# Linear attention with a SwiGLU FFN: another first load, corner matmuls and a new order of loads and attention steps in the first groups

## The chip, the cores and the metric

The kernel runs on one core of a Trainium2 chip. The metric is the device time of one execution in microseconds, lower is better. The kernel before takes 308.3 us, the median of 7 runs (307.77 to 308.72).

## The reference

q, k and v have 8 batches, 8 heads, 576 rows and 64 columns, all fp32. The output of a linear attention is laid out as 4608 tokens of 512 features and goes through a gated FFN with d_ff = 1536.

```python
q_p, k_p = phi(q), phi(k)                     # phi(x) = where(x > 0, x, exp(x) - 1) + 1
kv  = einsum('bhsd,bhse->bhde', k_p, v)
z   = sum(k_p, axis=2)
num = einsum('bhsd,bhde->bhse', q_p, kv)
den = einsum('bhsd,bhd->bhs', q_p, z)[..., None] + 1e-06
x   = (num / den).transpose(0, 2, 1, 3).reshape(4608, 512)
g   = x @ w_gate
out = (silu(g) * (x @ w_val)) @ w_out
```

## The kernel before

**Tiling.** A batch's 576 rows are 9 chunks j of 64 rows. A group g is 8 consecutive chunks (b, j), 512 tokens; there are 9 groups for the 8 batches, so group 0 holds chunks 0 to 7 of batch 0, and group 1 the last chunk of batch 0 and seven of batch 1. The kernel overlaps the attention of later batches with the FFN of a group. `lp` is a half of the heads (four heads, two SBUF pairs); `hh` and `e` pick 64-row halves of the array. d_ff is 12 blocks `fb` of 128.

**FFN.** L1 of a group computes, per fb, four gate matmuls and four value matmuls of 128x512 (`l1_mm`, lines 289 to 292), then ACT's silu and one DVE product into `hT` (`l1_gate`, 294 to 298). L2 multiplies hT with `wo` (line 450 for groups 0 and 1; line 506 for the later ones, which work on sums of weights `ws` and of hT; line 343 for the last two). `w_sum` (486) makes the weight sums, on POOL for the first blocks and on DVE in L1 of group 1.

**PSUM.** There are eight banks of 128x512 fp32: pG0-1, pV0-2, pX0-2. `l1_banks` (283) says which hold gate and value results; group 0 rotates four pairs, later groups two gate and three value banks.

**Attention of batch 0 (prologue, 680 to 713).** phi is kept as two terms, max(x, 0) and min(exp(x), 1), which are added by DVE (`k_sum`) for the first half of k only; elsewhere PE adds them in PSUM. `z0` sums phi(k) over rows with a ones matrix, `z0_copy` brings it to `zz`. `t0` transposes phi(q) by matmuls with an identity, `t0_copy` brings it to `qT`. `mm1` (166) computes v.k: for batch 0 in matmuls of 64 rows by 128 columns, of which two 64x64 blocks are used, for batch 1 as 64x64 corners. `r0_copies` (650) brings it to `R`, and `kv` (200) finds the blocks there. `corners` (258) multiplies zz or R with qT. `den0` takes logarithms and exponentials of the denominators on ACT; `num0` (671) multiplies numerators by them on DVE (`x0`, two products of 128x512) into `xT`, the FFN's input. The eight last-chunk (j = 8) products of batch 0, called d8 and n8, come in lines 856 to 869. `warm` (590) are matmuls without a use that keep PE running.

**Attention of batch 1 (first(), 796 to 808).** In L1 of group 0, after fb 3 a `block` computes exp and both terms of phi(k) for batch 1, and after fb 8 one for phi(q). The rest stands in lists between L2's steps: `t1` transposes phi(q), four and three chunks at a time with both head halves together, then `z0`, `den1`, `mm1`, `num1`, and for the last two chunks `t1(7, 9)`, `den2`, `num2`, `x2`. Some phi work of batch 2 stands there too (`exp_k`, `max_2`, `phi_k`, `exp_q`).

**What sets the order.** Everything is issued in the order of the program text to each engine's own queue; there is no planner. `at` (728) puts functions into numbered slots. All loads of q, k, v and the weights are DMAs issued by POOL that change fp32 to fp16 on the way; a half of q, k or v of batch 0 is 288 KB in fp16, a whole one 576 KB, a W1 block of 256 columns 256 KB for gate and the same for value, a third of wo 512 KB. They land in the order of issue. Outputs and transposes are DMAs of SyncE (SP).

The first loads are lines 570 to 577 (k half 0, q halves 0 and 1, k half 1, v halves, W1 columns 0 to 255), the next ones lines 714 to 725. The first L1 of group 0 for fb 0 and 1 is interleaved by contraction block i (lines 848 to 852), because xT 0 and 1 are there before xT 2 and 3:

```python
for i in range(4):
    for w in range(2):
        for fb in range(2):
            l1_mm(0, fb, w, i)
    if i == 0:
        r0_copies(1)
        num0(1)
```

L2 of group 0 (881 to 892) takes four fb for each of four token tiles t, three times.

Of the kernel before, what the change touches and what calls it, by code (L numbers as in the profile page):

```python
# [17 lines left out]
def kernel(  # L18
# [90 lines left out]
    def ld_w1(c0, c1):  # L109
        for (src, dst) in ((moe_w_gate, wg), (moe_w_val, wv)):  # L110
            nc.gpsimd.dma_start(out=dst[:, :, c0:c1], in_=src[:, c0:c1].rearrange("(c p) f -> p c f", p=P))

    def ld_w2(i):
        nc.gpsimd.dma_start(out=wo[:, 4 * i:4 * i + 4, :],
                            in_=moe_w_out[512 * i:512 * i + 512, :].rearrange("(c p) f -> p c f", p=P))
# [50 lines left out]
    def mm1(b, lp):  # L166
        if lp == 0:
            kvb[b] = ((pV[2], pX[0]), (pX[2], pV[2]), (pX[0], pX[1]), (pV[0], pG[0]), (pX[2], pV[2]))[min(b, 4)]
        for j in range(J):
            for (t, term_) in enumerate(terms_k(b, lp)):  # L170
                for hh in range(2):
                    rows = slice(C * hh, C * hh + C)
                    if b == 0:
                        nc.tensor.matmul(
                            out=kvb[b][hh][:, 256 * lp:256 * lp + P], lhsT=term_[rows, j, P * lp:P * lp + P],
                            rhs=v16[b][rows, 2 * lp:2 * lp + 2, D * j:D * j + D],
                            start=(j == 0 and t == 0), stop=(j == J - 1 and t == len(terms_k(b, lp)) - 1))
                        continue
                    for e in range(2):
                        w = D if b == 1 else D + 1  # L180
                        nc.tensor.matmul(  # L181
                            out=kvb[b][hh][D * e:D * e + D, 256 * lp:256 * lp + w],
                            lhsT=term_[rows, j, P * lp + D * e:P * lp + D * e + D],
                            rhs=v16[1][rows, 2 * lp + e, D * j:D * j + D] if b == 1 else vm[b % 2][rows, j, 2 * lp + e, :],
                            start=(j == 0), stop=(j == J - 1))
# [14 lines left out]
    def kv(b):  # L200
        c1 = D if b == 0 else 0
        return lambda i, e: R[b % 2][D * e:D * e + D, i, c1 * e:c1 * e + D]
# [80 lines left out]
    def l1_banks(g, fb):  # L283
        if g > 0:
            return pG[fb % 2], pV[fb % 3]
        i = fb % 4
        return (pG[0], pG[1], pX[0], pX[1])[i], (pV[0], pV[1], pV[2], pX[2])[i]
# [282 lines left out]
    load_0(k, k16, 0)  # L570
# [6 lines left out]
    ld_w1(0, 256)  # L577
# [25 lines left out]
    def k_max(lp):  # L603
        term(k16[0], kp[1], lp, 0.0, ALU.max)
# [14 lines left out]
    zb0 = (pG, (pX[2], pV[2]))  # L619

    def z0(b, lp):
        ts = terms_k(b, lp)
        for j in range(J):
            for t in ts:
                for hh in range(2):
                    rows = slice(C * hh, C * hh + C)
                    nc.tensor.matmul(out=zb0[b][hh][:, D * lp:D * lp + D], lhsT=t[rows, j, P * lp:P * lp + P],
                                     rhs=ones[rows, 0:D], start=(j == 0 and t is ts[0]),
                                     stop=(j == J - 1 and t is ts[-1]))

    def z0_copy(b, lp):
        for hh in range(2):
            nc.vector.tensor_scalar(out=zz[:, 2 * lp + hh, :], in0=zb0[b][hh][:, D * lp:D * lp + D], scalar1=1.0 / SC,
                                    scalar2=None, op0=ALU.mult)
# [15 lines left out]
    def r0_copies(lp):  # L650
        for hh in range(2):
            nc.vector.tensor_copy(out=R[0][:, 2 * lp + hh, 0:P], in_=kvb[0][hh][:, 256 * lp:256 * lp + P])
# [18 lines left out]
    def num0(lp):  # L671
        corners({2 * lp + e: nbank0[lp][e][:, :] for e in range(2)}, kv(0), 0, 0, 8, (lp,))
        for i in range(2 * lp, 2 * lp + 2):
            x0(nbank0[lp][i % 2][:, :], rr[:, i, :], xT[i][0][:, :])

    def t0_all(lp, t):
        for i in range(2):
            t0(pV[i], lp, 4 * i, 4 * i + 4, (t,))

    warm(42, pX[1])  # L680
    exp0(k16[0], ek, 0)
# [7 lines left out]
    z0_copy(0, 0)  # L689
    t0_all(0, 0)  # L690
    warm(2, pX[1])
    q_min(0)
    q_max(0, 1)
# [4 lines left out]
    warm(7, pX[1])  # L698
    den0(0)
    q_min(1)  # L700
    k_max(1)
    t0_all(1, 0)
    t0_all(1, 1)
    t0_copy(pV[0], 1, 0, 4, V)
# [3 lines left out]
    t0_copy(pV[1], 1, 4, 8, V)  # L708
# [5 lines left out]
    for c in (256, None, 512, 768, 1024):  # L714
        if c is None:
            ld_k(1)
        else:
            ld_w1(c, c + 256)
    ld_q(1)
    ld_w1(1280, 1536)  # L720
    ld_w2(0)
    ld_v(1)
    ld_w2(1)
    ld_w2(2)
# [9 lines left out]
    def phi_1(src, e, dst, lp):  # L734

        s = slice(2 * lp, 2 * lp + 2)
        nc.vector.tensor_scalar(out=e[:, s, :], in0=e[:, s, :], scalar1=1.0, scalar2=None, op0=ALU.min)
        d = dst[1][:, :, P * lp:P * lp + P].rearrange("p j (s d) -> p s j d", d=D)
        nc.vector.tensor_tensor(out=d, in0=d, in1=e[:, s, :].rearrange("p s (j d) -> p s j d", d=D), op=ALU.add)

    def t1(ps, j0, j1, eng):
        pt = ps[:, :].bitcast(FP16)
        for jj in range(j1 - j0):
            for lp in range(2):
                i = 2 * jj + lp
                nc.tensor.transpose(out=pt[:, P * i:P * i + P], in_=qp[1][:, j0 + jj, P * lp:P * lp + P],
                                    identity=id16[:, :])
        dst = qT[1][:, j0:j1, :, :].rearrange("p j l t -> p (j l t)")
        if eng == "A":
            nc.scalar.activation(out=dst, in_=pt[:, 0:2 * P * (j1 - j0)], func=AF.Copy, bias=0.0, scale=1.0)  # L750
        else:
            nc.vector.tensor_copy(out=dst, in_=pt[:, 0:2 * P * (j1 - j0)])
# [9 lines left out]
    def num1(lp):  # L762
        corners({2 * lp + e: nbank[e][:, 0:W7] for e in range(2)}, kv(1), 1, 0, 7, (lp,))
        for e in range(2):
# [8 lines left out]

    def num2():
        corners([nbank[m % 2][:, part1[m]] for m in range(4)], kv(1), 1, 7, 9)

    def x2():
        for m in range(4):
            x0(nbank[m % 2][:, part1[m]], r8[:, m % 2, part1[m]], xT[m][0][:, 0:W2])
# [6 lines left out]
    def block(src, e, dst):  # L786
        for lp in range(2):
            exp_(src, e, 1, lp)
            term(src[1], dst[1], lp, 0.0, ALU.max)
        for lp in range(2):  # L790
            phi_1(src, e, dst, lp)
# [4 lines left out]
    def first():  # L796
        sl = at(FB, [
            (3, lambda: block(k16, ek, kp)), (8, lambda: block(q16, eq, qp))])
        ln_set = lambda: nc.scalar.preload_act_table_set("natural_log_exp_and_others")
        w = at(13, [  # L800
            (0, lambda: t1(pX[0], 0, 4, A)), (0, ln_set), (1, lambda: t1(pX[1], 4, 7, V)), (1, lambda: z0(1, 0)),
            (1, lambda: z0(1, 1)), (1, lambda: z0_copy(1, 0)), (1, lambda: z0_copy(1, 1)),
            (2, lambda: den1(0)), (2, lambda: mm1(1, 0)), (2, lambda: mm1(1, 1)), (2, lambda: r1_copies()),
            (3, lambda: den1(1)), (3, lambda: num1(0)), (5, lambda: t1(pX[0], 7, 9, V)), (5, lambda: num1(1)),
            (6, lambda: den2()), (6, lambda: exp_k(2, 0)), (6, lambda: exp_k(2, 1)), (7, lambda: max_2(k16, kp, 0)),
            (7, lambda: max_2(k16, kp, 1)), (8, lambda: num2()), (9, lambda: phi_k(2, 0)), (9, lambda: exp_q(2, 0)),
            (11, lambda: exp_q(2, 1)), (12, lambda: x2()), (12, lambda: phi_k(2, 1))])
# [39 lines left out]
    part8 = [slice(C * (i // 2), C * (i // 2) + C) for i in range(4)]  # L847
    for i in range(4):
# [3 lines left out]
        if i == 0:  # L852
            r0_copies(1)
            num0(1)
        if i == 1:
            for lp in range(2):
                t0(pV[2][:, P * lp:P * lp + P], lp, 8, 9)
            for lp in range(2):
                t0_copy(pV[2][:, P * lp:P * lp + P], lp, 8, 9, V)
        if i == 2:  # L860
            d8 = [(pV[2], pX[0])[m % 2][:, part8[m]] for m in range(4)]
            n8 = [(pX[1], pX[2])[m % 2][:, part8[m]] for m in range(4)]
            corners(d8, zs, 0, 8, 9)
            ln0([pV[2][:, 0:P], pX[0][:, 0:P]], r8[:, :, 0:P])
            exp_neg(r8[:, :, 0:P])
    nc.scalar.preload_act_table_set("silu_and_others")
    corners(n8, kv(0), 0, 8, 9)
    for m in range(4):
        x0(n8[m], r8[:, m % 2, part8[m]], xT[m][1][:, 0:C])
# [11 lines left out]
    for i in range(3):  # L881
        if i < 2:
            for m in range(4):
                w_sum(nc.gpsimd, m, 2 * i, 2 * i + 2)
        for t in range(4):
            l2(0, t, 4 * i, 4 * i + 4)
            if (i, t) == (2, 1):
                l2_out(0, 1, V)
            for f in w[4 * i + t]:
                f()  # L890
            if i == 2 and t != 1:
                l2_out(0, t, V)
    for f in w[12]:
        f()
# [90 lines left out]
```

## Time and profile before

| | us |
|---|---|
| median of 7 runs (lowest, highest) | 308.3 (307.77, 308.72) |
| the profiled execution | 308.19 |
| its span in the trace | 306.4 |
| start of the first L1 matmul (line 291) | 16.38 |
| fb 2 of L1, group 0 | 21.76 |
| L2 of group 0 | 39.21 |
| L1 of group 1 | 54.13 |
| L2 of group 1 | 76.19 |
| L1 of group 2 | 87.74 |

The landings of the first loads, taken from the trace as the time when the last of the 16 DMA engines reports, in us:

| load | issued | landed |
|---|---|---|
| k half 0 | 1.26 | 5.40 |
| q half 0 | 2.12 | 8.03 |
| q half 1 | 3.13 | 9.47 |
| k half 1 | 3.84 | 10.90 |
| v halves | 4.55, 5.26 | 12.34, 13.76 |
| W1 0:256, gate and value | 6.03, 6.77 | 15.09, 17.44 |
| W1 256:512 | 7.50, 8.31 | 18.39, 19.73 |
| k(1) | 9.75 | 22.57 |
| W1 512:1280 | 11.19 to 18.68 | 23.92 to 30.59 |
| q(1) | 20.01 | 33.45 |
| W1 1280:1536 | 22.86, 24.20 | 34.79, 36.13 |
| wo 0:4 | 25.54 | 38.70 |
| v(1) | 26.87 | 41.50 |
| wo 4:8 and 8:12 | 28.23, 29.55 | 44.06, 46.72 |

Times in the trace count from the start of the span; the profiled execution's own time is longer than the span by what lies before its first and after its last instruction. The stages in the first table are where PE starts the named work; between two of them PE runs that stage and whatever attention work is put between its matmuls. Stages after 87.74 hold nothing that the diff changes.

### The profile page before, as it was taken

The page shows a single profiled execution, that of the slowest core. Times are in us where ns is not written, and L with a number is a line of the kernel's source. Part 1 is how long each engine was busy: PE and PEld are TensorE (multiplying, and loading weights), DVE is VectorE, ACT ScalarE, POOL GpSimd, SP SyncE. Part 2 cuts the span into 40 slices and gives each one's busy share as a digit, 9 for nine tenths or more (in the row PEclk, how much of TensorE's full clock was granted, in tenths as well). Part 3 has the DMA queues.
Part 4 walks back from the last instruction along what each step waited for, and adds up shares of the span by engine and source line. Part 5 has one row for each costly group of instructions (what it writes and reads, how often), then busy time and mean ns, then how long its engine had stood idle before and what let it go on. Part 6 is the DMA issues. An engine that isn't in the chain of part 4 may idle for free.

```text
span 306.4 us, 6673 instructions
## 1 busy us (share of the span) xinstructions
PE 298.5 (97%) x2587; PEld 183.2 (60%) x2587; DVE 251.2 (82%) x537; ACT 216.5 (71%) x335; POOL 48.3 (16%) x62
## 2 busy tenths in 40 slices
PE   8899999999999999999999999999999999999993
PEld 6644454444454486447744774468446888878882
DVE  3757757979977988998899889997999968968991
ACT  3759987969757878696869686968633478547930
POOL 8545386010200002000200000000000004001300
PEclk9999999999999999999999999999999999999999
DMA  7999999999496219921792133122312050033014
GB/s 100 194 199 199 203 207 208 258 215 165 67 226 131 49 28 161 213 51 29 128 238 47 36 69 71 28 54 52 87 26 54 10 131 0 2 68 72 0 37 103
DMA packets 41424, 32.29 MB, mean 105 GB/s; under 512 B 16352, under 2 KB 37280, under 8 KB 41392
## 3 DMA queue, kind: packets, MB, share of 16 engines
q0 software_dynamic: 20672, 18.94, 39.1%
q1 hardware_dynamic: 20560, 12.79, 17.8%
q8 instruction: 20, 0.33, 0.5%
q10 hardware_dynamic: 160, 0.13, 0.2%
q14 instruction: 12, 0.10, 0.1%
HBM read 37.75 MB, written 9.44 MB: 154 GB/s over the span
## 4 chain that ended last, share of the span: by engine, by line
PE 86%; issue 5%; DMA 3%; POOL 2%; ACT 2%; POOLq 0%; ACTq 0%
PE pV L291 22%; PE pG L291 21%; PE pX L506 14%; PE pV L506 4%; PE pV L343 4%; PE pG L343 4%; PE pG L450 4%; PE pV L450 3%; DMA wv<-in_moe_w_val_dram 3%; PE pX L291 3%; PE pX L343 1%; PE pV L264 1%; PE pX L181 1%; PE pV L411 1%; PE pX L264 1%
## 5 line engine op out<-in xcount | busy, mean ns | idle before, releaser
L291 PE MATMUL pV<-xT,wv 128*128 128x512 f16 x324 | 83.5, 379 | 0.5 <-DMA wv<-in_moe_w_val_dram 0.5
L291 PE MATMUL pG<-xT,wg 128*128 128x512 f16 x312 | 80.4, 379 | 0.1
L296 ACT ACTIVATE sil<-pG 128x512 f16<-128x512 f32 x78 | 45.9, 596 | 27.7 <-PE pG L291 18.0
L297 DVE SCALAR_TENSOR_TENSOR hT<-pV,sil 128x512 f16<-128x512 f32 x81 | 55.1, 687 | 12.0 <-ACT sil L296 7.0
L291 PEld LDWEIGHTS <-wv 128*128 128x128 f16 x336 | 32.8, 98 | 40.4 <-DMA wv<-in_moe_w_val_dram 1.0
L291 PEld LDWEIGHTS <-wg 128*128 128x128 f16 x336 | 32.2, 98 | 38.3 <-issue 0.7
L506 PEld LDWEIGHTS <-hs 128*128 128x128 f16 x336 | 32.5, 98 | 4.7 <-DVE hs L480 0.4
L383 POOL TENSOR_TENSOR hT<-prod,vm 128x512 f16<-128x512 f16 x6 | 6.9, 1153 | 132.0 <-ACT vm L370 132.0
L506 PEld LDWEIGHTS <-hT 128*128 128x128 f16 x252 | 24.3, 98 | 4.1
L506 PE MATMUL pX<-ws,hs 128*128 128x256 f16 x210 | 25.7, 273 | 0.0
L511 ACT ACTIVATE part<-pX 128x256 f32<-128x256 f32 x35 | 12.8, 381 | 13.2 <-PE pX L506 13.2
L95 POOL DMA_DIRECT2D k<-in_k_dram x7 | 5.2, 747 | 79.4 <-ACT part L511 58.8
L480 DVE TENSOR_TENSOR hs<-hT 128x512 f16<-128x512 f16 (+2 forms) x42 | 17.4, 418 | 0.2
L245 DVE TENSOR_TENSOR qp<-qp,rden 128x768 f16<-128x768 f16 x18 | 17.1, 949 | 0.0
L232 DVE TENSOR_REDUCE den<-prod 128x12 f32<-128x768 f16 x18 | 17.0, 943 | 0.0
L120 ACT ACTIVATE ek<-k 128x1152 f16<-128x1152 f16 x14 | 15.9, 1159 | 0.1
L120 ACT ACTIVATE eq<-q 128x1152 f16<-128x1152 f16 x14 | 15.6, 1168 | 0.0
L506 PE MATMUL pX<-wo,hT 128*128 128x256 f16 x126 | 15.2, 273 | 0.0
L450 PEld LDWEIGHTS <-hT 128*128 128x128 f16 x96 | 8.8, 98 | 10.3 <-issue 0.6
L155 ACT ACTIVATE vm<-v 128x1152 f16<-128x1152 f16 x12 | 14.1, 1177 | 0.0
L516 DVE SCALAR_TENSOR_TENSOR osb<-pX,part 128x256 f32<-128x256 f32 x28 | 10.7, 417 | 2.1 <-PE pX L506 1.9
L450 PE MATMUL pG<-wo,hT 128*128 128x512 f16 x48 | 11.7, 380 | 0.0
(183 smaller groups left out, 536.1 us busy)
## 6 DMA issues: line engine op xcount, KB each, us to landing
out_dram<-osb SPq DMA_DIRECT2D x64, 128.0 KB, 4.0
k<-in_k_dram POOLq DMA_DIRECT2D x7, 576.0 KB, 11.7
q<-in_q_dram POOLq DMA_DIRECT2D x7, 576.0 KB, 11.7
v<-in_v_dram POOLq DMA_DIRECT2D x7, 576.0 KB, 14.6
wg<-in_moe_w_gate_dram POOLq DMA_DIRECT2D x6, 256.0 KB, 11.7
wv<-in_moe_w_val_dram POOLq DMA_DIRECT2D x6, 256.0 KB, 11.9
wo<-in_moe_w_out_dram POOLq DMA_DIRECT2D x3, 512.0 KB, 15.8
out_dram<-osb SPq DMA_DIRECT2D x13, 64.0 KB, 2.0
```

What stands on the lines that cost most here:

```text
L120: nc.scalar.activation(out=e[:, s, :], in_=src[b % 2][:, s, :], func=AF.Exp, bias=0.0, scale=1.0)
L155: nc.scalar.activation(out=vm[b % 2][:, :, s, 0:D].rearrange("p j l d -> p l j d"), in_=v16[b % 2][:, s, :].rearrange("p l (j d) -> p l j ...
L232: nc.vector.tensor_reduce(out=den[:, HL * j0:HL * j1], in_=prod[:, 0:j1 - j0, :].rearrange("p j (l d) -> p (j l) d", d=D), axis=AX.X, op=A ...
L245: nc.vector.tensor_tensor(out=qv, in0=qv, in1=rden[:, HL * j0:HL * j1].unsqueeze(2).to_broadcast([P, HL * (j1 - j0), D]), op=ALU.mult)
L291: nc.tensor.matmul(out=ps[:, :], lhsT=src[:, i, P * fb:P * fb + P], rhs=xT[i][g % 2][:, :], start=(i == 0), stop=(i == 3))
L296: nc.scalar.activation(out=s[:, :], in_=pg[:, :], func=AF.Silu, bias=0.0, scale=1.0)
L297: nc.vector.scalar_tensor_tensor(out=hT[g % 2][:, fb, :], in0=pv[:, :], scalar=SC, in1=s[:, :], op0=ALU.mult, op1=ALU.mult)
L343: nc.tensor.matmul(out=dst[:, HN * e:HN * e + HN], lhsT=lhs, rhs=rhs, start=(n in (1, 2, 5) and e == 0 and c == 0), stop=(c == 1), skip_gr ...
L450: nc.tensor.matmul(out=pso[(g, t)][:, :], lhsT=hT[g % 2][:, fb, P * t:P * t + P], rhs=wo[:, fb, :], start=(fb == 0), stop=(fb == FB - 1))
L480: (eng or nc.vector).tensor_tensor(out=o, in0=a, in1=b, op=op)
L506: nc.tensor.matmul(out=(z if n in (2, 3, 5) else x)[:, 0:HD], lhsT=left(f), rhs=right(f), start=(f == 0 and n in (1, 2, 5)), stop=(f == HF ...
L511: nc.scalar.activation(out=part[:, 2 * i + tt, :], in_=(x if from_x else z)[:, 0:HD], func=AF.Copy, bias=0.0, scale=1.0 / SC)
```

## The change

The diff touches the loads, the attention of batches 0 and 1, and the banks of one stage.

- The first half of k is loaded by SyncE, in fp32 without a change of type, into the space of `ws` (`k32`); the exponential and the max read it there. POOL's first load is now q's first half.
- W1 columns 0 to 255 are loaded in row halves: gate rows 0:2, value rows 0:2, gate 2:4, value 2:4 (in blocks of 128 rows), four DMAs of half the size. wo is loaded as 0:2, 2:4, 4:8, 8:12.
- The later loads are in another order: W1 256 to 1279, then k(1), W1 1280, q(1), wo 0:2 and 2:4, v(1), wo 4:8, 8:12, k(2).
- Batch 0's v.k is computed as 64x64 corners like batch 1's: 108 matmuls where there were 54. The copies to R are 64 columns wide instead of 128. z0 of batch 0, the second half of t0 and the tails (j = 8) use other banks.
- In the prologue, `q_max(0, 1)` stands ahead of `q_min(0)`, the transposes of the second head half ahead of `den0(0)`, the tail transposes and copies ahead of `z0(0, 1)`; `num0` is cut into corners and `x00` products, and the R copies of the second half stand between two of them. The warm matmuls go from 51 to 41.
- The denominators of the last chunk follow `num0(1)` directly; its numerators (`num8`, `x8`) are moved into L2 of group 0.
- Batch 1's k block moves from after fb 3 to after fb 7, its q block from after fb 8 into L2 (slot 3), with exponentials written to `ws`'s space (`eq1`).
- L2 of group 0 has 16 steps instead of 12, two, two, four and four fb for each t, and the attention of batch 1 is spread over their slots. `t1` transposes one head half at a time (7 chunks), `t2` the last two chunks.
- Group 1's L1 rotates three gate banks (pG0, pG1, pX2) instead of two.

The core of the diff:

```diff
-    load_0(k, k16, 0)
+    k32 = ws[:, :, :, :].rearrange("p m f c -> p (m f c)").bitcast(FP32)[:, 0:2 * J * D].rearrange("p (l x) -> p l x", l=2)
+    nc.sync.dma_start(out=k32, in_=heads(k, 0)[:, 0:2, :])
...
-    ld_w1(0, 256)
+    ld_w1(0, 256, 0, 2)
+    ld_w1(0, 256, 2, 4)
...
-        term(k16[0], kp[1], lp, 0.0, ALU.max)
+        term(k16[0] if lp else k32, kp[1], lp, 0.0, ALU.max)
...
-                    if b == 0:
-                        nc.tensor.matmul(
-                            out=kvb[b][hh][:, 256 * lp:256 * lp + P], lhsT=term_[rows, j, P * lp:P * lp + P],
-                            rhs=v16[b][rows, 2 * lp:2 * lp + 2, D * j:D * j + D],
-                            start=(j == 0 and t == 0), stop=(j == J - 1 and t == len(terms_k(b, lp)) - 1))
-                        continue
                     for e in range(2):
-                        w = D if b == 1 else D + 1
+                        w = D if b < 2 else D + 1
...
-            return pG[fb % 2], pV[fb % 3]
+            return (pG[0], pG[1], pX[2])[fb % 3] if g == 1 else pG[fb % 2], pV[fb % 3]
...
+    q_max(0, 1)
+    q_min(0)
     t0_all(0, 0)
-    warm(2, pX[1])
-    q_min(0)
-    q_max(0, 1)
     t0_all(0, 1)
     t0_copy(pV[0], 0, 0, 4, V)
     t0_copy(pV[1], 0, 4, 8, A)
     exp0(k16[0], ek, 1)
-    warm(7, pX[1])
-    den0(0)
+    t0_all(1, 0)
+    warm(4, pX[1])
     q_min(1)
     k_max(1)
-    t0_all(1, 0)
     t0_all(1, 1)
-    t0_copy(pV[0], 1, 0, 4, V)
+    for lp in range(2):
+        t0(bank8[lp][:, 3 * P:4 * P], lp, 8, 9)
+    den0(0)
+    for i in range(2):
+        t0_copy(pG[i], 1, 4 * i, 4 * i + 4, V)
     k_min(1)
     mm1(0, 0)
     r0_copies(0)
-    t0_copy(pV[1], 1, 4, 8, V)
+    for lp in range(2):
+        t0_copy(bank8[lp][:, 3 * P:4 * P], lp, 8, 9, V)
     z0(0, 1)
     z0_copy(0, 1)
     num0(0)
     den0(1)
     mm1(0, 1)
-    for c in (256, None, 512, 768, 1024):
-        if c is None:
-            ld_k(1)
-        else:
-            ld_w1(c, c + 256)
+    x00(0, 0)
+    r0_copies(1)
+    x00(0, 1)
+    for c in (256, 512, 768, 1024):
+        ld_w1(c, c + 256)
+    ld_k(1)
+    ld_w1(1280, 1536)
     ld_q(1)
...
+        w = at(17, [
+            (3, lambda: z0(1, 0)), (3, lambda: z0(1, 1)), (3, q_block), (7, lambda: t1(0)), (7, lambda: mm1(1, 0)),
+            (7, lambda: mm1(1, 1)), (7, lambda: num8()), (7, lambda: r1_copies()), (7, lambda: x8()), (8, lambda: t1(1)),
+            (8, lambda: den1(0)), (9, lambda: num1(0)), (9, lambda: den1(1)), (9, lambda: x1(0)), (11, lambda: t2()),
+            (11, lambda: num1(1)), (11, lambda: x1(1)), (12, lambda: exp_k(2, 0)), (12, lambda: den2()),
+            (12, lambda: max_2(k16, kp, 0)), (12, lambda: max_2(k16, kp, 1)), (14, lambda: num2()),
+            (14, lambda: exp_k(2, 1)), (14, lambda: exp_q(2, 0)), (15, lambda: exp_q(2, 1)), (16, lambda: x2()),
+            (16, lambda: phi_k(2, 0)), (16, lambda: phi_k(2, 1))])
```

## The prediction

> **What bounds the kernel now.** I read the page first, then the chain of waits, then windows by stage, then the timeline of the first 20 us.
>
> ```profile
> PE 298.5 (97%) x2587; PEld 183.2 (60%) x2587; DVE 251.2 (82%) x537; ACT 216.5 (71%) x335; POOL 48.3 (16%) x62
> ...
> DMA  7999999999496219921792133122312050033014
> ```
>
> PE is busy 97% of the span, so an edit pays only if PE does less, or waits less, at a place where PE is last. The DMA row is full in its first ten slices (76 us). All that the diff touches lies there. By stage (start:end, length, then busy time of PE, PEld, DVE, ACT, POOL, clock, DMA share, GB/s):
>
> ```profile
> 16.38:21.76 5.38, 4.88 (x44) 1.86 (x40) 2.28 (x7) 2.32 (x5) 2.22 (x3) 1.00 1.33 204
> 21.76:39.21 17.45, 17.45 (x89) 7.95 (x82) 12.63 (x25) 16.42 (x20) 7.33 (x10) 1.00 1.36 201
> 39.21:54.13 14.92, 14.92 (x207) 7.34 (x206) 9.68 (x21) 12.29 (x18) 11.57 (x12) 1.00 1.22 207
> 54.13:76.19 22.06, 21.92 (x171) 10.08 (x169) 19.34 (x43) 18.39 (x27) 1.48 (x2) 1.00 1.12 217
> ```
>
> These are fb 0 and 1 of the first L1 with batch 0's corners; fb 2 to 11; L2 of group 0 with batch 1's attention; L1 of group 1. Outside the first, PE hardly idles: ten fb at 8 x 0.216 us are 17.28 of the second's 17.45. So time can come from the start (the prologue up to 16.38, where PE's 13.99 busy us are mostly warm-up matmuls, and the 5.38) or from fewer PE instructions. The chain agrees:
>
> ```profile
> 4.56 1.48 POOL v L98 x2
> 6.78 10.67 DMA wv<-in_moe_w_val_dram
> 21.84 0.97 PE pX L291 x4
> ```
>
> It begins with POOL's issues and the wv load. What else sets the start (timeline: start, duration, engine; in brackets the idle time before it and its releaser):
>
> ```profile
> 5.43 1.16 ACT L596 ACTIVATE ek<-k 128x1152 f16<-128x1152 f16 x1 [3.40 <-DMA k<-in_k_dram]
> 8.06 1.16 ACT L596 ACTIVATE eq<-q 128x1152 f16<-128x1152 f16 x1 [1.47 <-DMA q<-in_q_dram]
> ...
> 17.49 0.60 PE L291 MATMUL pV<-xT,wv 128*128 128x512 f16 x2 [0.50 <-DMA wv<-in_moe_w_val_dram]
> ```
>
> k's first half is awaited at 5.43, q's at 8.06; landing records put q's second half at 9.47, k's at 10.90, wv at 17.44. Each half load takes 1.43 us of a full pipe, each 256 KB 1.34. So the start is a queue of loads, with a DVE chain behind it.
>
> **What the Trainium skill says.** "DMA: Bandwidth & Descriptors", Specifications, gives a first byte after about 1 us for GpSimd's path and 0.6 for SyncE's. The trace has larger figures and the same gap:
>
> ```profile
> 2.00:3.00 1.00, 1.00 (x6) 0.67 (x5) 0.00 (x0) 0.02 (x1) 0.90 (x3) 1.00 0.17 16
> ...
> 212.00:212.50 0.50, 0.50 (x47) 0.46 (x40) 0.09 (x1) 0.12 (x1) 0.00 (x0) 1.00 0.00 0
> 212.50:213.00 0.50, 0.50 (x59) 0.46 (x44) 0.50 (x1) 0.50 (x2) 0.00 (x0) 1.00 0.87 193
> ```
>
> POOL's issue at 1.26 moves its first packet at 2.83 (1.57 later); SP's at 211.42 its first at 212.54 (1.12). The same page, "Issuing engines are not separate DMA queues", says that all issuers share 16 engines and interleave. The trace agrees: SP's output of 51.96, amid loads, moves nothing until 55.80. "VectorE: DVE Perf Modes", Mode 2×_2P, lets an fp32 tensor_scalar from SBUF make two results a cycle; no row here shows one. "TensorEngine Tiling (Array Packing)", Key Properties, has four independent 64x64 tiles and a drain at each change of mode; in this trace 72 such matmuls of batch 1 take 0.88 us, against 1.01 for batch 0's 36 of 64x128, and a change to or from 128 rows costs about 0.1.
>
> **The change, part by part.**
>
> *First k half by SP as fp32.* SP is free at 0.66, so first bytes come at about 0.66 + 1.12 = 1.8 instead of 2.83: the load stream starts 1.0 us earlier, and POOL's first issue (now q) goes out at 1.26 instead of 2.13. The read is the same; 576 KB are written where 288 were. If reading sets the pace the load takes 1.43 of the pipe; if writing, at the 201 GB/s that SP's outputs reach, 590/201 = 2.9. I take 1.43, since all cast loads read at twice that rate (2 x 206), so that every load after lands 1.0 us earlier; the other end makes them 1.0 - 1.47, 0.45 later. k_max on fp32: 1152 at two per cycle of 0.96 GHz is 0.60, plus the 0.15 that a fp16 one leaves over, 0.75 instead of 0.45 (1.35 if only one result a cycle). It ends beside ACT's exp (1.16), so at 0.75 it costs nothing, at 1.35 about 0.2.
>
> *Prologue.* q's second half lands at 9.47 - 1.0 = 8.5. Then DVE in its new order: q_max to 8.95, q_min to 9.4; PE's second transposes, then copies of 0.69 to 10.5; q_min, k_max (0.45 each) to 11.35; the two copies of head half 1 to 12.7; k_min 13.2; R copies (64 wide, 0.22 instead of 0.27) and tail copies 13.9. PE: z0(0,1) to 14.6, num0(0), den0(1), then mm1(0,1), whose 72 corners take 0.88 where 36 wide ones took 1.01, to 16.0. First L1 matmul 16.0 instead of 16.38: -0.35. The load gives 1.0, and 0.65 is spent on the tails and copies pulled ahead. PE's matmuls grow from 2587 to 2631 (54 more corners, 10 fewer warm ones); since the corners run together in quarters of the array, the growth costs nothing.
>
> *fb 0 and 1.* The 5.38 hold 16 x 0.216 = 3.46 of L1, 0.41 of num0(1), 0.39 of tail transposes, the wv wait of 0.50 and some 0.6 of 64-row corners and changes of mode. The W1 row halves land at about 13.4, 14.1, 14.8 and 15.5 (four of 0.67), so the wait goes, also at the straggler's extra 0.9, because only the first rows are needed first. Tails and num8 leave. New: the bank of wv fb 1 is free only when x00(0,1) is done, which stands behind the R copies that wait for mm1(0,1): 16.0 + 0.5 + 0.65 = 17.2 against PE's arrival at 16.65, a wait of 0.45 to 0.55. So 3.46 + 0.6 (num0(1) and batch 0's eight corners of denominators) + 0.45 = 4.5; fb 2 starts at 20.5 instead of 21.76: **-1.2**.
>
> *fb 2 to 11.* 10 x 1.728 as before. Reordered loads: W1 up to 1024 comes by 26.2, ahead of need (fb 8 at 30.9); k(1) at 29.0 for a block now behind fb 7 (30.9, cover 1.9); the set ahead of wo 2:4 is the same, so it lands at 38.70 - 1.0 = 37.7, wo 0:2 before it, L2's start being 37.8. v(1) lands at 40.5, used at 42; wo 4:8 at 43.1, used at about 43.5: cover 0.4, as thin as before (44.06 against 44.26). Without the earlier start these covers shrink together with the earlier PE, so they cost nothing more.
>
> *L2 of group 0.* PE gets num8's 8 corners (0.14) and one more change of mode (0.1). t1(0) waits for phi of q(1): q_block's DVE work is 2 x 0.45 + z copies 0.7 + two mins and sums, about 2.4 us from slot 3, against four slots of 0.43 and z0's 0.6: 0.2 late. Queued behind t1(0) on PE are mm1(1) and the corners. **+0.45** (0 if that wait vanishes, +1.0 if ACT's three Ln/exp pairs come late as well).
>
> *POOL.* w_sum of rows 0 to 2 now waits until eq1 is read (about 43.5, was 38.77); behind it on POOL is k(3)'s issue, 48.7 to 52.7. The pipe is full until v(2) lands at 55.6, so k(3) still queues: nothing, cover 2.9 us.
>
> *L1 of group 1.* Of its 0.14 idle and some 0.3 of late starts (gate bank waiting for silu), a third gate bank takes part: **-0.15** (0 to -0.3). DVE enters it with a phi pair more, 1.2 us. The cover: the last hT is done at 77.31 and used by the twelfth matmul at 78.57; qT's last piece lands at 82.8, used at 83.9.
>
> Sum: -1.2 + 0.45 - 0.15 = **-0.9**. Against the profiled execution's 308.19 (span 306.4) that is 307.3; it lies 0.1 under the median of the runs, so 308.3 - 0.9 = **307.4**.
>
> **The rivals.** *Gain handed back.* DVE is already 19.34 of 22.06 busy in group 1's L1; with 1.2 us more the covers of 1.1 to 1.3 are spent, PE waits 0.3 to 0.6 around 69 to 84, where a wait shows already:
>
> ```profile
> 67.39 1.08 issue
> 69.12 1.02 PE pG L291 x4
> ```
>
> That gives 308.0. Against it: the covers are just long enough.
>
> *Larger gain.* q's first half came late in one of 16 engines only (8.03, median engine 6.62); if SP's load spreads that, q lands up to 0.6 earlier still: 306.8.
>
> *Slower: the fp32 load holds the pipe.* SP's packets share 16 engines with POOL's from 2.83 on, and if writing sets the pace (2.9 us) everything after is 0.45 later than before instead of 1.0 earlier. Then fb 2 starts at 20.5 + 1.45 = 21.95, L2 keeps its +0.45, and with the group 1 gain lost to DVE: 308.3 + 0.2 + 0.45 = **308.9 to 309.0**. It decides from about 2.3 us of pipe for this load. For it: 200 GB/s is all that SP's fp32 outputs show, and that late output at 51.96. Against: mixed stretches run at 298 GB/s and more.
>
> **How the numbers follow.** Forecast 0.48 (307.0 to 307.8), handed back 0.22, larger gain 0.13, slower 0.17. About 0.2%, 0.6 us, is what a measurement of this kernel can tell from no change; the bounds are 307.7 and 308.9. Faster: 0.41 of the forecast's, all 0.13, 0.01 of handed back: 0.55. Slower: 0.13 of the last. Same: 0.32. The range is 306.7 to 309.0.
>
> **What would show it.** Right: the first exp starts before 5.2 and the first eq before 7.5; L1 starts near 16.0 with no DMA behind a PE wait; fb 2 at 20.3 to 20.7; L2 of group 0 about 15.4 long; group 1's L1 at most 22.0. Wrong: k lands after 5.5 or q's second half after 9.2 (the pipe is held); L2 over 15.9; PE waiting for DVE in group 1.

## The result and the profile after

The changed kernel takes 309.86 us (median of 12 runs, 309.11 to 312.01), against 308.35 for the kernel before (30 runs). The ratio is 1.006, 95% interval 1.0047 to 1.0073: slower by 0.6%, where 307.4 was forecast. Ratios, here and below, leave out executions more than 1.5% above the fastest of their kernel (one in run 4, four in run 6). The profiled execution took 310.08, with a span of 308.3 against 306.4.

By stages, in the same view as before (start:end, length, busy time of PE, PEld, DVE, ACT, POOL, clock, DMA share, GB/s); the first row is the prologue:

```profile
0.00:18.59 18.59, 13.42 (x251) 10.32 (x251) 9.62 (x27) 10.35 (x12) 13.70 (x23) 0.91 1.11 178
18.59:23.02 4.43, 4.13 (x39) 1.75 (x29) 2.24 (x5) 3.08 (x6) 2.51 (x4) 1.00 1.45 197
23.02:40.28 17.26, 17.26 (x81) 7.83 (x80) 10.07 (x17) 11.20 (x16) 5.91 (x8) 1.00 1.29 204
40.28:56.23 15.95, 15.62 (x215) 7.37 (x214) 12.33 (x29) 13.31 (x17) 10.20 (x10) 1.00 1.07 186
56.23:77.98 21.75, 21.74 (x169) 10.08 (x169) 19.58 (x42) 18.12 (x27) 3.48 (x5) 1.00 1.13 203
```

| stage | before | after | difference | forecast |
|---|---|---|---|---|
| up to the first L1 matmul | 16.38 | 18.59 | +2.21 | -0.35 |
| fb 0 and 1 | 5.38 | 4.43 | -0.95 | -0.9 |
| fb 2 to 11 | 17.28 | 17.26 | 0 | 0 |
| L2 of group 0 | 14.93 | 15.95 | +1.02 | +0.45 |
| L1 of group 1 | 22.05 | 21.75 | -0.30 | -0.15 |
| all after it | 230.4 | 230.3 | 0 | 0 |

(The numbers of before are cut at PE's own matmul starts, up to 0.17 earlier than the windows in the prediction.) The loss is the prologue and, smaller, L2 of group 0. The mean clock that PE was granted in the prologue is 0.91 of full speed. In the page's row of slices (PEclk, tenths of full speed) the second slice has a 7:

```profile
PE   7689999999999999999999999999999999999993
...
PEclk9799999999999999999999999999999999999999
```

The chain of waits (start, length, what) has a new piece. Its first long load is q's now, not wv's, and later PE stands still with the reason "issue", which means that it waited for nothing that the profile shows:

```profile
2.42 6.85 DMA q<-in_q_dram
12.11 0.97 PE pG L638 x8
17.31 0.94 issue
```

The timeline of PE has the place (start, duration, engine, line, instruction, then idle time before it). This standstill, called the stop from here on, is in the middle of batch 0's second corners, between two matmuls of one loop that need nothing new:

```profile
17.11 0.20 PE L175 MATMUL pX<-v,kp 64*64 64x64 f16 x2
18.25 0.22 PE L175 MATMUL pV<-v,kp 64*64 64x64 f16 x2 [0.94 <-issue]
...
18.60 0.39 PE L284 MATMUL pG<-xT,wg 128*128 128x512 f16 x1
```

The DMA view of 15.5 to 17.0 (queue, packets, MB, share) shows one packet that is no data of the kernel's: on queue q8, 16 KB of instructions. It started at 15.80. Below it stands q8's row of the page, for the whole span:

```profile
q0 software_dynamic: 568, 0.28, 140.2%
q8 instruction: 1, 0.02, 4.1%
...
q8 instruction: 20, 0.33, 0.4%
```

That these are PE's instructions is inferred from the count: twenty packets for PE's 2631 matmuls and 2631 weight loads, one for some 263, spread over the whole span. Such a packet is called a fetch below.

So two things happened that the prediction had no term for. The clock was halved from 11.11 to 14.52, after PE had idled at 7.33 to 8.39 and 9.00 to 10.18. And PE stopped for 0.94, up to 2.44 us after the start of a fetch. That it waits for these instructions is a reading that the experiments have to bear out, since the packet itself is on record for only about 0.98 us (4.1% of 16 engines' 1.5 us), so until 16.8, and the profile doesn't show what fills the rest. The Trainium skill has something on both. "TensorE: Matmul & The Clock Gate", What's actually happening, gives half clock after an idle window of about 3413 ns. The length agrees (the drop lasted 3.41), but no whole window was idle here: PE was busy for 1.55 of the 3.41 us before the drop. "Runtime: NRT & Kernel Launch", Instruction fetch mechanics, says that instructions come in blocks of 16 KB by DMA, with a cost mostly hidden. The block's size agrees; that it is hidden doesn't hold for this kernel.

The profiled execution is one of five with a mean clock of 0.994 over the span; these took 310.08 to 312.01. The other seven, with 0.996 to 0.999, took 309.11 to 309.89. Since 3.41 us at half clock take 0.0055 off the mean of such a span, these seven can't hold a whole drop of that length. So the median of 309.86 is a loss without the halved clock of the profiled execution.

### The profile page after: what moved, and what is told of

It reads as the page before. It is cut to its first block, busy times and chain, and to the rows that moved or that the text cites. A ratio compares the mean times of both kernels' runs of the same rounds, so it can differ in the third digit from the quotient of the medians.

```text
span 308.3 us, 6764 instructions
## 1 busy us (share of the span) xinstructions
PE 297.7 (97%) x2631; PEld 182.9 (59%) x2631; DVE 252.3 (82%) x537; ACT 214.2 (69%) x333; POOL 50.0 (16%) x64
## 4 chain that ended last, share of the span: by engine, by line
PE 86%; issue 5%; DMA 2%; DVE 2%; ACT 2%; POOL 1%; POOLq 0%
PE pV L284 23%; PE pG L284 21%; PE pX L499 14%; PE pV L499 4%; PE pV L336 4%; PE pG L336 4%; PE pX L284 4%; PE pV L443 3%; PE pG L443 2%; DMA q<-in_q_dram 2%; PE pX L175 1%; PE pV L257 1%; PE pX L336 1%; PE pV L175 1%; PE pV L404 1%
## 5 line engine op out<-in xcount | busy, mean ns | idle before, releaser
L284 PE MATMUL pG<-xT,wg 128*128 128x512 f16 x296 | 76.3, 379 | 0.3 <-DVE osb L453 0.3
L289 ACT ACTIVATE sil<-pG 128x512 f16<-128x512 f32 x74 | 43.5, 597 | 29.5 <-PE pG L284 20.3
L238 DVE TENSOR_TENSOR qp<-qp,rden 128x768 f16<-128x768 f16 x18 | 17.1, 949 | 0.0
L120 ACT ACTIVATE eq<-q 128x1152 f16<-128x1152 f16 x12 | 13.3, 1170 | 0.0
L443 PE MATMUL pV<-wo,hT 128*128 128x512 f16 x48 | 12.0, 380 | 0.0
## 6 DMA issues: line engine op xcount, KB each, us to landing
wo<-in_moe_w_out_dram POOLq DMA_DIRECT2D x2, 512.0 KB, 15.9
```

Source lines behind the costliest of these rows:

```text
L120: nc.scalar.activation(out=e[:, s, :], in_=src[b % 2][:, s, :], func=AF.Exp, bias=0.0, scale=1.0)
L238: nc.vector.tensor_tensor(out=qv, in0=qv, in1=rden[:, HL * j0:HL * j1].unsqueeze(2).to_broadcast([P, HL * (j1 - j0), D]), op=ALU.mult)
L284: nc.tensor.matmul(out=ps[:, :], lhsT=src[:, i, P * fb:P * fb + P], rhs=xT[i][g % 2][:, :], start=(i == 0), stop=(i == 3))
L289: nc.scalar.activation(out=s[:, :], in_=pg[:, :], func=AF.Silu, bias=0.0, scale=1.0)
L443: nc.tensor.matmul(out=pso[(g, t)][:, :], lhsT=hT[g % 2][:, fb, P * t:P * t + P], rhs=wo[:, fb, :], start=(fb == 0), stop=(fb == FB - 1))
```

## The experiments

My theory after the traces: the 64x64 corners use up PE's instructions faster than a fetch brings new ones, and the stop follows; the clock is a second, separate loss; L2's +1.02 is a third. The rivals are named with each run. "More under" or "over" another kernel means the difference of the medians, in us.

**1. Fill PE's idle gaps, with the same count of instructions.**

```diff
-    warm(37, pX[1])
+    warm(21, pX[1])
+    warm(8, pX[1], 512)
...
+    warm(4, pX[1], 512)
     q_max(0, 1)
     q_min(0)
     t0_all(0, 0)
+    warm(4, pX[1], 512)
     t0_all(0, 1)
```

> The changed kernel with PE's idle gaps at 7.3 and 9.0 us filled: eight warm matmuls of 512 columns stand there, and eight of 256 fewer ahead of them, so that the number of PE instructions up to the second transposes is the same. Theory (idle PE halves the granted clock from 11.1 to 14.5, and instructions that come late stop PE for 0.94 at 17.3, independently): the clock stays 1.00, first L1 about 0.5 earlier than 18.6, the stop of 0.9 on PE before the first L1 stays; time about 309.3, and the runs spread less. Rival (the clock is the whole loss of the prologue, the stop is one of its consequences): first L1 at 16.9 or earlier, time 308.0. Rival (the clock costs nothing since loads set the start): first L1 stays at 18.6.

Measured: 311.21 (6 runs), ratio 1.0081 (1.006 to 1.0102), no gain at all. The prologue's clock stayed at 1.00 and PE came to the corners 0.65 earlier, but only to stop longer. Timeline of this kernel:

```profile
18.23 0.22 PE L175 MATMUL pV<-v,kp 64*64 64x64 f16 x2 [1.57 <-issue]
18.58 0.39 PE L284 MATMUL pG<-xT,wg 128*128 128x512 f16 x1
```

PE goes on at 18.23 with the clock full and at 18.25 with it halved, and the first L1 matmul is at 18.58 and 18.59: what the prologue's clock lost was hidden behind the fetch. The stop in turn cost the clock in the next stage, fb 0 and 1 of this kernel:

```profile
18.58:24.50 5.92, 5.63 (x38) 2.10 (x29) 2.24 (x5) 2.84 (x6) 2.92 (x4) 0.71 1.45 197
```

It took 5.92 instead of 4.43. A halved clock beside L1 is thus worth 1.5. The runs agree: four, the profiled one among them, have a mean clock of 0.994 and took 311.17 to 311.61, the two with 0.997 and 1.00 took 309.96 and 309.58. So the theory's 309.3 was near where the clock held, and missed the median, because it had no term for a clock lost to the stop. The first rival (308.0) failed. The last rival had the place of the first L1 matmul right, 18.6, but for another reason: PE came early and stood.

**2. The same gaps filled with sixteen more matmuls of 256 columns**, so 32 more PE instructions ahead of the corners:

```diff
+    warm(8, pX[1])
     q_max(0, 1)
     q_min(0)
     t0_all(0, 0)
+    warm(8, pX[1])
     t0_all(0, 1)
```

> The changed kernel with the same gaps filled by sixteen more warm matmuls of 256 columns, so that PE's queue has 32 instructions more before the second transposes. Theory (the stop of 0.94 at 17.3 is a fetch of PE instructions, asked for when PE is some 115 instructions from its end, which the 64x64 corners use up faster than a fetch of about 2.4 us amid loads): the fetch is asked for earlier in the idle part, the stop goes, clock stays 1.00: first L1 at about 17.1, time 308.3. Rival (the stop is a wait for data): it stays as in the run with wide warm matmuls, first L1 about 18.1, time 309.3.

Measured: 308.19 (13 runs), ratio 1.0006 (0.9997 to 1.0015): 1.7 under the changed kernel, level with the one before. No stop; the first L1 matmul at 16.25. The fetch started at 13.37, 2.4 earlier than in the changed kernel, while PE waited for DVE. Of the forecast's own steps nothing is changed in this kernel, and its stages are what the forecast should have given:

```profile
16.25:20.69 4.44, 4.14 (x38) 1.76 (x29) 2.24 (x5) 4.17 (x8) 3.12 (x5) 1.00 1.45 197
...
37.95:53.90 15.95, 15.68 (x215) 7.45 (x214) 12.21 (x29) 13.19 (x17) 10.20 (x10) 1.00 1.20 209
53.90:75.64 21.74, 21.74 (x169) 10.04 (x169) 19.46 (x42) 18.11 (x27) 3.46 (x5) 1.00 1.13 203
```

fb 2 starts at 20.69 (forecast 20.5), and L2 costs 15.95 as in the changed kernel, so it isn't an effect of the late start. Runs 1 and 2 fill the same gaps; only run 2 has more instructions, and only there the stop is gone. The rival "a wait for data" failed.

**3. The first half of k by POOL again.** Edit: `load_0(k, k16, 0)` for SP's load, exp and max on k16.

> The changed kernel with the first half of k loaded by POOL with the change to fp16, as before the change, all else kept. Theory (the fp32 load takes 2.4 us of the pipe, so that all later loads come only 0.2 earlier): q lands at 8.0 and 9.5, only 0.2 later than with SP's load; k is there at 5.4 and PE's warm matmuls end closer to the first use, so PE idles less and the clock may stay up: time at most 0.2 over the changed kernel's, or below it by up to 0.6. Rival (SP's load is worth its 1.0 and something else delays q): q lands at 8.8 and 10.2, time 0.8 more.

Measured: 310.64, ratio 1.0076 (1.0057 to 1.0094). q landed at 7.14 and 9.42, against 7.84 and 9.26: the second half as the theory of the held pipe said (9.5), and not as its rival (10.2). The time is 0.8 over the changed kernel's, as the rival had it, but the intervals of the two ratios overlap, and PE still stopped, 1.58 us up to 18.50. So the time says nothing on the load itself; run 10 does.

**4. The start of the change alone in the kernel before.**

> The kernel before with only the start of the change: SP's fp32 load, row halves of W1, corners for batch 0, the new order of the prologue and of fb 0 and 1; loads after that, L1 and L2 of group 0 and the banks of group 1 as before, the last chunk's numerators after fb 1. Theory (the start costs 1.25 up to fb 2, the rest of the change 0.7: 1.02 in L2 less 0.30 in L1 of group 1): time 309.4 to 309.6. Rival (the start alone is the loss, and L2's part is an effect of the later start): 309.9. Rival (the loss is in the rest): 308.5.

Measured: 310.06 (6 runs), ratio 1.0048 (1.0031 to 1.0066), which lies between the theory's 309.5 and the rival's 309.9 and excludes neither; the third, 308.5, is out. PE stopped at the same matmul, up to 17.98. In its profiled execution, by far the longest of the six (315.43), phi(q) of batch 1 fell beside POOL's sums of weights (its sum took 1.59 us; k's sum of the same size in the prologue of before took 0.76) and PE waited 2.72 for it in L2. That is one execution, and L2's price isn't read from it.

**From here on** the kernels leave out the 18 DMA transposes that bring phi(q) of batches 2 to 7 into qT; the numerators of these batches use what batches 0 and 1 left there. They are compared with a control that leaves them out too.

**5. The control.**

> Control: the kernel before without the 18 DMA transposes that bring phi(q) of batches 2 to 7 into qT; the numerators of these batches use what batches 0 and 1 left there. All up to 66 us is as before. Every theory: first L1 at 16.4, fb 2 at 21.8, L2 of group 0 at 39.0, L1 of group 1 at 54.0; the time is within 0.6 of 308.2, since no transpose was waited for, and it is the base for the other kernels that leave them out.

Measured: 307.70 (21 runs), ratio 0.9988 (0.9981 to 0.9995). fb 2 to 11 took 17.48 instead of 17.28, L2 of group 0 and L1 of group 1 the same as before within 0.1, and all after it 0.4 less. The first L1 matmul is at 16.14, fb 2 at 21.10, since wv landed at 16.78 and not at 17.44. The wait of 0.5 for it is thus not in every execution.

**6. The corners alone**, in the control: the change's `mm1`, `kv` and `r0_copies`, nothing else.

> The control (DMA transposes left out) with one part of the change alone: batch 0's v.k as 64x64 corners (54 more matmuls, R copies 64 wide). Theory (PE stops at its 223rd matmul until a fetch of instructions lands, about 2.45 us after it starts, where small matmuls bring it there too soon): a stop of 0.5 to 1.5 appears on PE at the 223rd matmul, inside the second corners of batch 0, none in the control; first L1 at 17.0 to 17.6 instead of 16.4; part of it is covered by the wait for wv that is there anyway, so the time is 0.3 to 0.8 over the control. Rival (corners are only the cheaper form): first L1 at 16.2, time at most that of the control.

Measured: 308.62 (22 runs), ratio 1.0027 (1.0007 to 1.0048), 0.9 over the control, somewhat more than the forecast 0.3 to 0.8. Seven of the runs lie apart at 311.8 to 314.4; the other fifteen, 307.84 to 308.90, have a median of 308.38. The profile is of one of the seven (311.77):

```profile
17.21 0.26 PE L175 MATMUL pX<-v,kp 64*64 64x64 f16 x2 [1.69 <-issue]
17.83 0.61 PE L283 MATMUL pG<-xT,wg 128*128 128x512 f16 x1
```

One part of the change brings the stop into a kernel that had none, after the 223rd matmul as forecast; the first L1 matmul, at 17.83, is later than the forecast 17.0 to 17.6. The clock halved after it (from 17.20), and PE later waited 1.41 for phi(q) of batch 1. The profile is no picture of the fifteen shorter runs: that they have the stop too is not shown, only that corners cost time in them as well.

**7. The changed kernel without the corners.**

```diff
+                    if b == 0:
+                        nc.tensor.matmul(
+                            out=kvb[b][hh][:, 256 * lp:256 * lp + P], lhsT=term_[rows, j, P * lp:P * lp + P],
+                            rhs=v16[b][rows, 2 * lp:2 * lp + 2, D * j:D * j + D],
...
```

> The changed kernel without DMA transposes, and with batch 0's v.k back in 64x128 matmuls (54 fewer), all else kept. Theory (as for the corners alone): no stop at the 223rd matmul, since that now falls into L1 of 128x512 matmuls; the clock still falls to half in the prologue, since PE idles as before; first L1 at about 17.6 to 17.9 instead of 18.6, so the time is 0.7 to 1.0 over the control instead of 1.5 to 1.9. Rival (the stop belongs to something else in the start): it stays at some place ahead of L1, and the time is 1.5 to 1.9 over the control.

Measured: 308.72, ratio 1.0017 (1.0004 to 1.003), 1.0 over the control. No stop, as the theory had it. That the time agrees with it too (0.7 to 1.0) is partly luck: the first L1 is at 16.92, better than the 17.6 to 17.9 expected, since the clock stayed full although PE idled 1.34 in one piece at 8.2. fb 2 starts at 21.47, and what is left of the loss is mostly L2: 15.96.

**8. The start mended, L2 and the order of loads as before.** Edit: run 4's kernel with run 2's sixteen warm matmuls, wo's first third in two loads, three gate banks in L1 of group 1.

> The control (DMA transposes left out) with the start of the change (SP's fp32 load, W1 row halves, corners, order of the prologue), sixteen more warm matmuls, wo's first third as two loads, and three gate banks in L1 of group 1; k and q blocks, order of loads and L2 of group 0 as before. Theory (the start then wins 1.1 up to fb 2, L2 of group 0 costs its old 14.93, the third bank wins 0.30): 1.0 to 1.4 under the control. Rival (with an earlier L2 the old order makes phi(q) of batch 1 collide with POOL's sums of weights or with late loads): the control's time or more.

Measured: 306.98 (8 runs), ratio 0.997 (0.9957 to 0.9983): 0.7 under the control, in the direction of the theory but short of its 1.0 to 1.4. Its stages (fb 0 and 1, L2 of group 0, L1 of group 1):

```profile
16.97:21.69 4.72, 4.42 (x45) 1.81 (x37) 2.24 (x5) 4.45 (x8) 2.26 (x4) 1.00 1.31 203
38.96:53.84 14.88, 14.88 (x207) 7.34 (x206) 9.49 (x21) 12.12 (x17) 11.96 (x12) 1.00 1.22 207
53.84:75.59 21.75, 21.75 (x170) 10.08 (x169) 19.06 (x41) 18.22 (x27) 1.56 (x3) 1.00 1.08 208
```

L2 is back at 14.88, with the third bank's 0.30 kept. In this execution the start gave nothing: q's second half landed at 9.06, and fb 2 began at 21.69, later than in the control's profile (21.10). The two profiled executions took about the same, 307.29 and 307.25, so the profiles don't show where the rest of the medians' 0.7 lies.

**9. A base for three more: run 2's kernel without transposes.**

> The changed kernel without DMA transposes, with the sixteen more warm matmuls: base for the three kernels beside it. Every theory: as with the transposes, first L1 near 16.3, fb 2 near 20.7, L2 of group 0 takes 15.9, and the time is the control's (307.7) within 0.3.

Measured: 308.13, ratio 0.9996 (0.9985 to 1.0007), 0.4 over the control instead of within 0.3. No stop; first L1 at 17.18, q's second half at 8.82. Run 2's kernel, which differs in the transposes alone, had 16.25: single executions can differ by that much here.

**10. k by POOL on that base.**

> The same base with the first half of k by POOL with the change to fp16. This prices SP's load where no fetch stops PE. Theory (SP's load makes q land 0.2 to 0.9 earlier, which the order of DVE passes on): first L1 0.3 to 0.9 later than the base's, time 0.3 to 0.9 more. Rival (the pipe is held by the fp32 bytes and nothing is won): equal within 0.2.

Measured: 308.44, ratio 1.001 (1.0002 to 1.0017), 0.3 over the base, the low end of the forecast. The intervals overlap, so that SP's load wins anything is likely, and not shown. q's second half landed 0.8 later (9.61), the first L1 only 0.09 later, where 0.3 to 0.9 was expected.

**11. The instructions moved without filling the gaps**: the last 16 of the first 37 warm matmuls as 32 of half the width.

```diff
-    warm(37, pX[1])
+    warm(21, pX[1])
+    warm(32, pX[1], 128)
```

> The changed kernel without DMA transposes, with the last sixteen of the first 37 warm matmuls cut into 32 of 128 columns: 32 more PE instructions ahead of everything, in the same time, and the idle gaps of PE at 7.3 and 9.0 left as they are. Theory (two independent things): no stop at the 223rd matmul, but the clock still halves for 3.4 us after 11; first L1 at 17.2 to 17.7, time 0.8 to 1.4 over the base with more warm matmuls. Rival (only the fetch counts, the halved clock hides behind loads): first L1 at 16.3 to 16.6, time within 0.3 of the base. Rival (the clock makes the stop): the stop stays, time 1.5 to 2.0 over the base.

Measured: 307.93, ratio 0.9995 (0.9984 to 1.0006), level with the base. No stop, fetch at 13.60, first L1 at 16.38. PE still idled 1.13 before the second transposes, once and not twice, and the clock held. The changed kernel's ratio is 1.006; besides the transposes, which gave the control 0.0012, nothing differs from it but thirty-two instructions earlier in the program, and the loss of the prologue is gone. The numbers are those of the rival "only the fetch counts", but its other half wasn't tested: what the halved clock of the prologue alone would cost stays open, since it didn't come. In L2 of group 0 the earlier start gave something back: it took 16.40, with PE waiting 0.26 for wo and 0.44 for DVE.

**12. L2's last wait**: `(pX[2], pG[0], pG[1])[fb % 3]` for group 1's gate banks.

> The base with more warm matmuls, with the three gate banks of L1 of group 1 in the order pX2, pG0, pG1 instead of pG0, pG1, pX2, so that the first gate matmul doesn't wait for DVE to bring L2's second tile out of pG0. Theory (0.17 to 0.31 of L2's 1.02 are this wait): no idle PE ahead of L1 of group 1, time 0.15 to 0.35 under the base. Rival (DVE is late anyway and the next bank is waited for): the wait moves to another matmul of the same stage, time as the base.

Measured: 307.71 (22 runs), ratio 0.9985 (0.9978 to 0.9992), 0.4 under the base. L2 of group 0 took 15.49 (15.96 in the base), no idle ahead of L1 of group 1:

```profile
38.35:53.84 15.49, 15.45 (x215) 7.38 (x214) 11.87 (x28) 12.85 (x17) 9.73 (x9) 1.00 1.21 208
```

All fourteen profiles on one table, with the start of the fetch on q8 and the starts of PE's 223rd and 224th matmul, counted in the trace:

| kernel | fetch | 223rd | 224th | from fetch to 224th |
|---|---|---|---|---|
| before | 15.24 | 20.11 | 20.42 | 5.2 |
| control (5) | 14.37 | 19.45 | 19.76 | 5.4 |
| no corners (7) | 15.29 | 20.82 | 21.04 | 5.7 |
| after | 15.80 | 17.11 | 18.24 | 2.4, stop |
| wide warm (1) | 15.71 | 16.46 | 18.23 | 2.5, stop |
| k on POOL (3) | 16.08 | 16.72 | 18.50 | 2.4, stop |
| start only (4) | 15.54 | 16.22 | 17.98 | 2.4, stop |
| corners only (6) | 14.99 | 15.32 | 17.20 | 2.2, stop |
| more warm (2) | 13.37 | 15.71 | 15.72 | 2.3 |
| start mended (8) | 13.91 | 16.43 | 16.44 | 2.5 |
| base (9) | 13.56 | 16.65 | 16.65 | 3.1 |
| base, k on POOL (10) | 14.29 | 16.73 | 16.73 | 2.4 |
| small warm (11) | 13.60 | 15.76 | 15.90 | 2.3 |
| gate order (12) | 13.77 | 16.11 | 16.18 | 2.4 |

In no profile does PE start its 224th matmul less than 2.2 us after the fetch started. Those five that stop come to the 223rd 0.3 to 1.3 after the fetch. Those that come there 2.3 or later have no stop; run 11, which comes there 2.16 after it, has 0.14 between the two matmuls.

## Why the prediction was wrong, step by step

**The step that failed** is the prologue's sum to "First L1 matmul 16.0", and in it the sentence that 44 more matmuls cost nothing, since the corners run together in quarters of the array. That priced their execution and not their supply. The execution was priced rightly: the 72 corners of the second half start within 0.73 us in run 2, the 36 wide matmuls in run 7 within 0.96. But the 108 corners put more instructions ahead of L1 and use them up faster than the 64x128 ones, so that the end of the fetched instructions, which before fell into L1 where each matmul lasts 0.216, fell into the second corners. In the profiled execution the stop is 0.94 of the 2.6 missed. Half of the 2.6 was lost before it, up to z0(0, 1), which started at 15.20 where 13.9 was forecast: q landed at 9.26 instead of 8.5, and work on the halved clock was slower (eight transposes of 128 columns in 1.03 instead of 0.62). But this part was not what set the time: run 1 won 0.65 of it back and stopped the longer. Without the stop (runs 2 and 8 to 12, all with corners) the first L1 matmul came at 16.25 to 17.27, in run 2 with z0(0, 1) at 13.98. Runs 6 and 7 show the cause from both sides: corners alone bring the stop, and without them it goes. Runs 1, 2 and 11 show that it hangs on the count of instructions ahead and not on PE's idle gaps.

**The loads.** "Every load after lands 1.0 us earlier" was mis-sized. The prediction's own sign of it, q's second half after 9.2, came in the changed kernel's profile (9.26), though in no other with SP's load. SP's load did land at 4.3 instead of 5.4, but q's second half landed at 8.59 to 9.26, mean 8.93, in the nine profiles with SP's load, and at 9.11 to 9.61, mean 9.35, in the five with POOL's: 0.4 earlier. The windows of the changed kernel show where the 1.0 went:

```profile
2.00:3.00 1.00, 1.00 (x6) 0.69 (x5) 0.23 (x1) 0.03 (x1) 0.90 (x3) 1.00 0.93 316
3.00:4.00 1.00, 1.00 (x6) 0.75 (x5) 0.00 (x0) 0.00 (x0) 1.00 (x3) 1.00 1.11 267
4.00:5.00 1.00, 1.00 (x10) 0.81 (x9) 0.65 (x1) 0.65 (x1) 1.00 (x2) 1.00 0.82 71
5.00:6.00 1.00, 1.00 (x11) 0.90 (x10) 0.62 (x2) 0.51 (x1) 1.00 (x2) 1.00 1.06 159
```

SP's 590 KB move at 316 and 267 GB/s (bytes written, the last column). POOL's queue has its first packet at 3.61 and begins slowly, with 71 GB/s, as it did before (16 from 2 to 3 us, 157 from 3 to 4). Its slow start came mostly after SP's load and not beside it. By 6.0 the changed kernel has 249 KB of q beside k, against 529 KB of all loads in the kernel before, which is 1.84 halves against 1.79. The fp32 load's pipe cost lay between the two ends that the prediction had set, and the rival "the fp32 load holds the pipe" was half right. It gave the right direction of the time (308.9 to 309.0) for a reason that didn't decide: with the stop gone the kernel is at 308.2 with the same load. The rival "larger gain" did not come either: q's first half landed at 7.42 in the mean of the nine profiles, against 7.55 in the five.

**fb 0 and 1**: right, mechanism and size (4.43 against 4.5), the new wait behind x00(0, 1) at 0.29 instead of 0.45 to 0.55.

**L2 of group 0**: the sign was right, the term mis-sized, 1.02 for 0.45; L2 came out at 15.95, over the 15.9 named as a sign of being wrong. PE's work other than L2's own matmuls, counted from each start to the next, grew by 0.4 (4.48 against 4.07), where 0.14 and 0.1 were counted. A wait of 0.30 ahead of L1 of group 1 was not in the sum at all. Timeline of DVE and PE there:

```profile
54.18 1.41 DVE L594 TENSOR_SCALAR kp<-k 128x1152 f16<-128x1152 f16 x1
55.51 0.68 DVE L453 TENSOR_SCALAR osb<-pG 128x512 f32<-128x512 f32 x1
...
56.24 0.59 PE L284 MATMUL pG<-xT,wg 128*128 128x512 f16 x2 [0.30 <-DVE osb L453]
```

The eviction of tile 1's bank stands on DVE behind a max that took 1.41 there instead of 0.45, and group 1's first gate matmul wants that bank. The chain of waits comes there through ACT's logarithms and exponentials of batch 1's denominators, then DVE:

```profile
48.93 0.95 ACT rr L658
49.88 1.06 ACT rr L655 x2
50.96 0.96 ACT rr L658
51.94 1.16 DVE xT L661 x2
53.70 1.89 DVE kp L594 x2
```

So part of the case that the prediction had put at +1.0, ACT's pairs coming late, did come. Run 12 takes the wait away, and its median is 0.4 lower, though the two intervals (0.9978 to 0.9992 against 0.9985 to 1.0007) overlap. The remaining 0.3 or so may be changes of mode and t1's wait; no run splits it.

**L1 of group 1**: the third bank won 0.30, the bound that was named. The rival "gain handed back" did not come: PE is busy 21.74 of 21.75 there, and k(3), issued by POOL at 55.2, was waited for by nobody there.

**The forms of cost that held**: DVE's max of fp32 took 0.81 (0.75 forecast), SP's first bytes came by 1.9 (1.8), the wait for wv is gone in every profile with row halves. As an estimate from these figures, 2.4 of the 2.5 between forecast and measurement are 1.7 of stop (the changed kernel against run 2), 0.57 of L2 and 0.25 of the start (16.25 in run 2 for 16.0), less 0.15 that the third bank gave beyond its term. The control's 307.70 against run 8's 306.98 puts the parts that held at about 0.7, the third bank's 0.30 among them.

## What to carry to other kernels

Count instructions, not only time. In these runs a burst of small matmuls used up PE's instructions, and a fetch that started too late stopped PE where no data was missing, with "issue" as the only reason in the timeline. Look for a 16 KB packet on an instruction queue ahead of such a stop, and put more instructions ahead of the burst, so that the fetch starts earlier; 32 did it here, whether they filled idle time (run 2) or not (run 11). And when the first load is moved to another queue, ask where the slow start of the old queue goes: here POOL's came after SP's load, and 1.0 us of earlier start became 0.4 of earlier landing.

## What the runs showed of the hardware that was not expected

- From the start of a 16 KB instruction fetch to the next PE instruction that needed it: 2.2 to 2.5 us in five kernels that stopped, amid loads that fill the DMA engines. The packet's own record takes 0.9 to 1.0 of it; what the rest is stays open. Whether it would be shorter with an idle pipe was not tried.
- The stop is fixed to a count of PE's instructions, not to time: 224 weight loads and 223 matmuls had run in all five, at 15.3 to 17.1 us, though the programs ahead of it differ.
- A stop of 1.57 to 1.69 us on PE was followed by 3.41 us at half clock in three of the four profiles that have one (runs 1, 4 and 6, not 3); the stop of 0.94 in the changed kernel was not. Idle gaps of 1.06 and 1.17 within 3 us were followed by it in the changed kernel's profile, one of 1.34 in run 7 was not.
- A DVE tensor_scalar of 128x1152 in fp16 took 0.44 at 11.91 in the changed kernel, with POOL idle, and 1.41 at 54.18, beside a POOL tensor operation that ran from 53.90 to 55.27.
